# A batch's DFT folded fully on POOL and taken through DRAM, its load moved ahead of a weight load, and the last stores split over two queues

## The chip, the cores and the metric

The kernel runs on one core of a Trainium2 chip. The metric is the device time of one execution in microseconds; for the kernel before, the median of four runs is 630.72 us (630.26 to 631.77). Five engines work side by side: TensorE (PE), VectorE (DVE), ScalarE (ACT), GpSimd (POOL) and SyncE (SP, which only issues DMAs here). Each takes its own instructions strictly in the program's order and waits on semaphores for the others.

## The reference

```python
x: float32 [8, 3008, 256]
y = fft(fft(x, axis=1), axis=2).real            # real part of a 2-D DFT, per batch
g = y @ w_gate;  v = y @ w_val                  # 256 -> 1536, over 24064 tokens
out = (gelu(g) * v) @ w_out                     # 1536 -> 256, float32
```

## The kernel before, in words

The eight batches go one after the other. Each has two parts: a DFT that prepares the tokens, and the feed-forward part (FFN).

**FFN.** The tokens of a batch are worked on in three chunks (512, 512 and 481 columns). A column stands for a token and for its mirror token, since the real part of the DFT splits into an even part E and an odd part O that the two share with opposite signs. For each chunk and each of the 12 slices of 128 of the hidden width there is one *slot*; a batch has 36 slots (NS), the program 288, and a slot takes about 2.1 us. In a slot TensorE does the gate matmuls (L659 into ps_g), those of the value (L659 into ps_v) and up to two pieces of four output matmuls (L748) that belong to the chunk before. ACT applies GELU (L675, L684), DVE combines the values (L703, L719, L721), and POOL multiplies the mirrored half (L723 into h_sb), one slot later. An output piece needs h_sb of four slices: its last piece for the first 128 columns of a chunk comes three slots after the chunk's last slice, two after the L723 of that slice. ACT copies finished output tiles (L768) and SP stores them, four DMAs a tile (L653).

**DFT of the next batch.** It runs in the slots of the batch before. The input rows are loaded in forward and in mirrored order (the mirrored ones by indirect gathers that POOL issues, L158) and *folded* on POOL: sums of forward and mirrored rows and channels (L215, L216, L219). Five pieces, PIECES, cover the 17 row groups. For batches 2 to 7 the fold works in f32 on x_raw, writes ab_sb, and two more operations (L223, `combine`) give the sum and the difference as bf16 in eo_sb. Then comes `s1t`: 17 matmuls of 256 columns with G as weights (L545), ACT writes the result to S_sb (L548), SP writes S_sb to DRAM in two DMAs (L556) and reads it back as Z_sb in another arrangement (L567). From Z_sb, `tp_y`, `tp_e` and `tp_o` (L611, L581) make E and O of the batch in EO_sb, and `tp_rows` copies one row through DRAM (yrow, L625 and L627).

Batches 0 and 1 are different (`half = b < 2`): their rows are cast to bf16 by the load (xb), and the fold writes its sums directly into eo_sb, without `combine`. Their first stage is `s1`, 34 matmuls of 96 columns (L504) into A_sb (ACT, L510), and `ch` puts the halves together with 24 matmuls of 256 columns against the signed identity II (L526), six evictions into Z_sb (ACT, L531). Batch 0 does all this before and early in its own slots, batch 1 in slots 6 to 33: fold operations in POOL slots 6 to 10 and 14 to 18, `s1` in slots 13, 14 and 16 to 21, `ch` and the `tp` functions spread over 22 to 33.

**Order.** The order is written out by hand: `opening` emits the loads and the first DFT; `plan` fills two tables, `pool` (fold operations) and `fill` (everything else beside the FFN), by slot; `feed` walks the slots. In a slot the order is gate, last slot's second gate part, value, the first of two output pieces, the slot's POOL operations, last slot's second value part with its L723, the second output piece, the slot's `fill` entries. For the first chunk, `sooner` in `feed` says in which slot its first six output pieces go.

In `opening` POOL issues, in order, the casts of x(0), eight casts of gate and value weights (w_raw), two casts of the output weight (Wo_sb, L428), and then the six casts and gathers of x(1) into xb (L179, L158). SP's forward load of x(2) follows as soon as the buffer of x(0) is free.

**The end.** In the very last chunk each output tile of 128 tokens and one sign is copied alone: sign 0 by DVE (L761), stored by SP, sign 1 by ACT (L764), stored from ACT's own queue, two DMAs each.

Of the kernel before, what the change touches and what calls it, by code (L numbers as in the profile page):

```python
# [28 lines left out]
def kernel(  # L29
# [98 lines left out]
    def gelu_tile():  # L128
        return work([128, 2, TOK], BF16, "gelu", 5, "gelu_sb")
# [43 lines left out]

    xb, stage = {}, {}

    def cast_forward(b, j0, nj):
# [9 lines left out]

    def fold_ops(b, j0, nj, eng):
        st = {}  # L190
        half = b < 2

        def fwd(c0, pat):
            if b == 0 and j0 not in range(1, 9):
                return _sub(stage[0], [[C, nj]] + pat, (j0 - 9 if j0 else 8) * C + c0, part_num=NP)
            if half:
                return _sub(xb[b], [[C, nj]] + pat, j0 * C + c0, part_num=NP)
            return _sub(raw_tile(FORWARD), [[C, nj]] + pat, j0 * C + c0, part_num=NP)

        def mir(c0, pat):  # L200
            if half:
                return _sub(xb[b], [[-C, nj]] + pat, (NJ + 16 - j0) * C + c0, part_num=NP)
            return _sub(raw_tile(MIRROR), [[-C, nj]] + pat, (16 - j0) * C + c0, part_num=NP)

        def ab(q, c0, pat):
            if half:
                return _sub(eo, [[C, nj]] + pat, j0 * C + q * 128 + c0)
            return _sub(st["ab"], [[C, nj]] + pat, q * 128 + c0)

        up, down = [[1, 127]], [[-1, 127]]  # L210

        def first():
            if not half:
                st["ab"] = ab_tile()
            eng.tensor_tensor(ab(0, 0, [[128, 2]]), fwd(0, [[128, 2]]), mir(0, [[128, 2]]), op=ALU.add)  # L215
            eng.tensor_tensor(ab(0, 1, up), fwd(1, up), mir(255, down), op=ALU.add)  # L216

        def second():
            eng.tensor_tensor(ab(1, 1, up), mir(1, up), fwd(255, down), op=ALU.add)  # L219

        def combine(g, op):
            def run():
                eng.tensor_tensor(  # L223
                    _sub(eo, [[C, nj], [1, 128]], j0 * C + g * 128),
                    ab(0, 0, [[1, 128]]), ab(1, 0, [[1, 128]]), op=op)
            return run

        if half:
            return [first, second]
        return [first, second, combine(0, ALU.add), combine(1, ALU.subtract)]  # L230
# [405 lines left out]
    def store(b, gi, sub, sign, osb_half, queue):  # L636
        segs = [c for c in cols[gi] if c[0] // 128 == sub]
        m = min(128, chunk_len[gi] - sub * 128)
        for off, k2, w in segs:
            p0 = off - sub * 128  # L640
            lo, hi = (1, w - 1) if sign and k2 == 0 else (0, w)
            if sign:
                t0 = T - k2 - N2 * (hi - 1)
                p1 = m - p0 - hi
            else:
                t0 = k2 + N2 * lo
                p1 = p0 + lo
            dst = ap_replace(
                out,
                ap=[[N2 * C, hi - lo], [1, C]],  # L650
                offset=out.offset + (b * T + t0) * C,
            )
            queue.dma_start(out=dst, in_=_sub(osb_half, [[1, C]], 0, part_start=p1, part_num=hi - lo))  # L653

    def ffn_work(b):
        cstate = {}
# [127 lines left out]
    def opening():  # L784
        stage[0] = stage_tile()
        xb[0] = xb_tile(0)
        for j0, nj, at in ((9, 8, 0), (0, 1, 8)):
            nc.sync.dma_start(
                out=_sub(stage[0], [[1, nj * C]], at * C),
                in_=ap_replace(x, ap=[[32 * C, NPX], [1, nj * C]], offset=x.offset + j0 * C))  # L790
        pool_consts()
        index_consts(0)
        cast_mirror(0, 9, 8)
        pool_consts2()
        cast_mirror(0, 5, 4)
        cast_forward(0, 1, 8)
        index_consts(1)
        cast_mirror(0, 0, 1)
        cast_mirror(0, 1, 4)
        for f0, n in ((0, 256), (256, 256), (512, 512), (1024, 512)):  # L800
            load_w(f0, n)
        for q in range(2):
            load_wo(q)
        xb[1] = xb_tile(1)
        cast_forward(1, 9, 8)
        cast_mirror(1, 9, 8)
        cast_forward(1, 0, 9)
        for j0, nj in ((5, 4), (1, 4), (0, 1)):
            cast_mirror(1, j0, nj)
        idle = gelu_tile()[:, 0, :]  # L810
        nc.vector.memset(one[:, 0:1], 1.0)
        sin_table()
        nc.vector.memset(idle, 0.0)

        def warm(n):

            ps = psum("o")
            for _ in range(n):
                nc.tensor.matmul(ps[:, :], idle[:, 0:128], idle[:, :], start=True, stop=True)  # L819

        def fold_piece(j0, nj):
            for f in fold_ops(0, j0, nj, nc.vector):
                f()

        vec_consts()
        vec_fills()
        warm(7)
        g_phases()
        t_columns()
        t_phases()  # L830
        g_rows(9, 7)
        t_reduced()
        vec_consts2()
        identities()
        cw_phases()
        g_ends()
        cw_magnitude()
        vec_fills2()
        g_rows(1, 8)
        t_sin()  # L840
        cw_sin()
        gelu_table()
        warm(6)
        fold_piece(9, 4)
        s1(0, 2, 0)()
        s1(0, 2, 1)()
        warm(8)
        fold_piece(13, 4)
        cw_rest()
        fold_piece(5, 4)  # L850
        s1(0, 1, 0)()
        s1(0, 1, 1)()
        warm(2)
        fold_piece(0, 1)
        s1(0, 3, 0)()
        s1(0, 3, 1)()
        fold_piece(1, 4)
        t_write()
        s1(0, 0, 0)()
        s1(0, 0, 1, "V")()  # L860
        minus = []
        make_w(0, 0, 256, m_at=minus, tag="o")()
        ch(0, 0)()
        ch(0, 1, "V")()
        make_w(1, 0, 256, m_at=minus, tag="g")()
        tp_e(0, 0, 0, "V", tag="v")()
        tp_e(0, 0, 1, "A", tag="v")()
        minus[0]()
        minus[1]()
# [7 lines left out]
    def plan():  # L877
# [16 lines left out]
        for i, f in enumerate(early):  # L894
            at(fill, (7, 8, 9, 10, 11, 12, 13, 14, 15, 16)[i], f)

        ops = []
        for piece in PIECES:
            ops += fold_ops(1, *piece, nc.gpsimd)
        slot_of = [6, 7, 8, 9, 10, 14, 15, 16, 17, 18]  # L900
        for s, f in zip(slot_of, ops):
            at(pool, s, f)
        s = 12
        for jg, piece in ((2, 1), (1, 2), (0, 3), (3, 4)):
            for g in range(2):
                s = max(s + 1, slot_of[2 * piece + 1] + 2)
                at(fill, s, s1(1, jg, g))
        last1 = s
        for k, s in ((0, 8), (1, 9), (2, 9)):
            at(fill, s, lambda k=k: load_part(2, k, (load_forward,)))  # L910
        for k, s in ((0, 18), (1, 19), (2, 19)):
# [8 lines left out]
                if i % each == each - 1:  # L920
                    at(fill, s + 1, tp_rows(b, i // each))

        items = []
        for gi in range(NG):
            items += [ch(1, 2 * gi), ch(1, 2 * gi + 1), tp_y(1, gi), tp_e(1, gi), tp_o(1, gi)]
        spread(1, items, last1 + 1, NS - 3)
        for b in range(2, B):
            s0 = (b - 1) * NS
            ops = []
            for j0, nj in PIECES:  # L930
                ops += fold_ops(b, j0, nj, nc.gpsimd)
            per = len(ops) // 5
            first, n = {2: (s0 - 13, 29), 3: (s0 - 19, 30)}.get(b, (s0 - 22, 32))
            slot_of = [first + i * n // len(ops) for i in range(len(ops))]
            for s, f in zip(slot_of, ops):
                at(pool, s, f)
            if b + 1 < B:
                for k, piece in ((0, 1), (1, 3), (2, 4)):
                    at(fill, slot_of[piece * per + 1] + 1, lambda b=b, k=k: load_part(b + 1, k))
            s = s0 - 9  # L940
            for i, (jg, piece) in enumerate(((2, 1), (1, 2), (0, 3), (3, 4))):
                ready = slot_of[piece * per + per - 1] + 2
                for g in range(2):
                    s = max(s + 1, ready)
                    at(fill, s, s1t(b, jg, g))
                if i == 2:
                    at(fill, s + 1, z_write(b, 0, 12))
                if i == 3:
                    at(fill, s + 1, z_write(b, 12, 4))
            at(fill, s + 2, z_read(b))  # L950
            items = []
            for gi in range(NG):
                items += [tp_y(b, gi), tp_e(b, gi), tp_o(b, gi)]
            assert s + 7 < s0 + NS - 10
            spread(b, items, s + 7, s0 + NS - 3)
        return fill, pool

    def feed():
# [6 lines left out]
        pend, before = [], None  # L965

        first = works[0]
        sooner = {6: [first[0]], 7: [first[3]], 10: [first[1]], 11: [first[4]], 13: [first[2]], 14: [first[5]]}
        works[0] = first[6:]
        for i, (parts, fc) in enumerate(blocks):  # L970
            if fc == 0 and i:
# [58 lines left out]
```

## Time and profile before

| | |
|---|---|
| median of the runs | 630.72 us (630.26 to 631.77) |
| the profiled execution | 631.84 us, of which its span is 630.1 us |
| TensorE busy, granted clock | 619.6 us (98% of the span), 1.00 |
| DVE, ACT, POOL busy | 578.4, 430.7, 494.5 us |
| L526 on TensorE (ps_dft<-II, A_sb) | 44 recorded, 20 of them of batch 0 |
| L504 on TensorE (from eo_sb) | 68, 34 of them of batch 1 |
| L545 on TensorE (from eo_sb, G) | 102, 17 for each of batches 2 to 7 |
| bytes moved by DMA | 63.83 MB, mean 101 GB/s |

A profile row gives the start in the span, the busy time, the engine, the line of the kernel, the operation, output<-inputs with their shapes, and the count; in brackets the idle time just ahead and what ended it. Matmuls overlap in a pipeline, so a row's busy time is longer than the distance to the next. The first slices of the span are the opening, slot 0 starts at 20.6 us.

### The profile page before, as it was taken

The page shows a single profiled execution, that of the slowest core. Times are in us where ns is not written, and L with a number is a line of the kernel's source. Part 1 is how long each engine was busy: PE and PEld are TensorE (multiplying, and loading weights), DVE is VectorE, ACT ScalarE, POOL GpSimd, SP SyncE. Part 2 cuts the span into 40 slices and gives each one's busy share as a digit, 9 for nine tenths or more (in the row PEclk, how much of TensorE's full clock was granted, in tenths as well). Part 3 has the DMA queues.
Part 4 walks back from the last instruction along what each step waited for, and adds up shares of the span by engine and source line. Part 5 has one row for each costly group of instructions (what it writes and reads, how often), then busy time and mean ns, then how long its engine had stood idle before and what let it go on. Part 6 is the DMA issues. An engine that isn't in the chain of part 4 may idle for free.

```text
span 630.1 us, 13007 instructions
## 1 busy us (share of the span) xinstructions
PE 619.6 (98%) x4284; PEld 408.7 (65%) x4284; DVE 578.4 (92%) x941; ACT 430.7 (68%) x848; POOL 494.5 (78%) x500
## 2 busy tenths in 40 slices
PE   8999999999999999999999999999999999999997
PEld 4456666666666666666666666666666666666666
DVE  7589889999899999999999999999999999999992
ACT  5867777767766667666776767766776766666661
POOL 8358889989997998879998799969988555555551
PEclk9999999999999999999999999999999999999999
DMA  9951525534454352632636335633222332221123
GB/s 179 222 98 27 149 63 144 137 103 138 119 146 107 90 140 68 169 113 72 154 93 157 93 68 138 153 91 104 56 54 54 89 95 55 52 52 38 43 51 80
DMA packets 52505, 63.83 MB, mean 101 GB/s; under 512 B 7783, under 2 KB 48218, under 8 KB 50042
## 3 DMA queue, kind: packets, MB, share of 16 engines
q1 hardware_dynamic: 45238, 47.23, 29.3%
q0 software_dynamic: 6608, 15.29, 11.3%
q8 instruction: 33, 0.54, 0.4%
q10 hardware_dynamic: 592, 0.49, 0.3%
q14 instruction: 34, 0.28, 0.2%
HBM read 38.86 MB, written 29.38 MB: 108 GB/s over the span
## 4 chain that ended last, share of the span: by engine, by line
PE 93%; DVE 2%; ACT 2%; issue 1%; DMA 1%; POOL 0%; POOLq 0%; DVEq 0%; ACTq 0%
PE ps_o L748 38%; PE ps_g L659 29%; PE ps_v L659 19%; PE ps_dft L545 2%; PE ps_dft L581 2%; PE ps_o L819 1%; DMA EO_sb<-yrow 1%; PE ps_dft L526 1%; PE ps_dft L442 1%; ACT gelu_sb L675 1%; PE ps_dft L611 0%; PE ps_g L748 0%; PE ps_v L389 0%; ACT gelu_sb L684 0%; DVE v_sb L721 0%
## 5 line engine op out<-in xcount | busy, mean ns | idle before, releaser
L723 POOL TENSOR_TENSOR h_sb<-gelu_sb,v_sb 128x512 bf16<-128x512 bf16 (+1 forms) x280 | 319.6, 1144 | 103.7 <-DVE v_sb L721 93.6
L748 PE MATMUL ps_o<-Wo_sb,h_sb 128*128 128x256 bf16 (+1 forms) x2232 | 334.6, 273 | 0.0
L748 PEld LDWEIGHTS <-h_sb 128*128 128x128 bf16 (+1 forms) x2304 | 228.8, 100 | 111.4 <-POOL h_sb L723 1.2
L675 ACT ACTIVATE gelu_sb<-ps_g 128x512 bf16<-128x512 f32 (+1 forms) x288 | 169.5, 589 | 98.1 <-PE ps_g L659 97.7
L659 PE MATMUL ps_g<-EO_sb,W_sb 128*128 128x512 bf16 (+1 forms) x864 | 231.1, 376 | 1.6 <-ACT gelu_sb L684 1.1
L703 DVE SCALAR_TENSOR_TENSOR ve_sb<-EB_sb,yw,ps_v 128x512 f32<-128x512 bf16 (+1 forms) x280 | 206.2, 736 | 27.1 <-PE ps_v L659 25.9
L659 PE MATMUL ps_v<-EO_sb,W_sb 128*128 128x512 bf16 (+1 forms) x576 | 214.0, 376 | 0.5 <-DVE W_sb L450 0.4
L719 DVE TENSOR_TENSOR h_sb<-gelu_sb,ps_v 128x512 bf16<-128x512 bf16 (+1 forms) x280 | 189.6, 677 | 1.1 <-ACT gelu_sb L684 0.7
L659 PEld LDWEIGHTS <-W_sb 128*128 128x128 bf16 x1440 | 136.6, 98 | 81.5 <-issue 2.1
L721 DVE SCALAR_TENSOR_TENSOR v_sb<-ve_sb,ps_v 128x512 f32<-128x512 f32 (+1 forms) x280 | 187.2, 669 | 0.0
L684 ACT ACTIVATE gelu_sb<-ps_g 128x512 bf16<-128x512 f32 (+1 forms) x288 | 169.0, 587 | 0.0
L768 ACT ACTIVATE out_sb<-ps_o 128x512 f32<-128x512 f32 x92 | 54.9, 597 | 34.5 <-PE ps_o L748 34.5
L223 POOL TENSOR_TENSOR eo_sb<-ab_sb 94x512 bf16<-94x512 f32 (+1 forms) x60 | 66.6, 1110 | 0.1
L591 ACT ACTIVATE EO_sb<-ps_dft 128x512 bf16<-128x512 f32 (+1 forms) x44 | 26.0, 590 | 23.4 <-PE ps_dft L581 21.5
L548 ACT ACTIVATE S_sb<-ps_dft 96x512 bf16<-96x512 f32 x48 | 28.2, 587 | 11.3 <-PE ps_dft L545 11.3
L219 POOL TENSOR_TENSOR ab_sb<-x_raw,x_raw 94x508 f32<-94x508 f32 (+1 forms) x30 | 33.0, 1099 | 0.0
L216 POOL TENSOR_TENSOR ab_sb<-x_raw,x_raw 94x508 f32<-94x508 f32 (+1 forms) x30 | 32.9, 1097 | 0.0
L545 PE MATMUL ps_dft<-eo_sb,G 94*96 94x256 bf16 x102 | 19.2, 274 | 0.1
L158 POOL DMA_INDIRECT x_raw<-in_x_dram,idx x18 | 17.0, 942 | 2.8 <-issue 0.8
L581 PE MATMUL ps_dft<-TP,Z_sb 128*128 128x128 bf16 (+1 forms) x184 | 17.9, 218 | 0.7 <-DVE Z_sb L533 0.7
L581 PEld LDWEIGHTS <-Z_sb 128*128 128x128 bf16 x192 | 14.6, 98 | 2.8 <-DVE Z_sb L533 1.4
L158 POOL DMA_INDIRECT xb<-in_x_dram,idx x8 | 7.7, 966 | 9.0 <-DMA w_raw<-in_moe_w_gate_dram 7.0
(148 smaller groups left out, 191.9 us busy)
## 6 DMA issues: line engine op xcount, KB each, us to landing
out_dram<-out_sb SPq DMA_DIRECT2D x361, 64.0 KB
x_raw<-in_x_dram SPq DMA_DIRECT2D x10, 768.0 KB
Z_sb<-z SPq DMA_DIRECT2D x6, 768.0 KB
z<-S_sb SPq DMA_DIRECT2D x6, 576.0 KB
EB_sb<-yrow SPq DMA_DIRECT2D x14, 128.0 KB
x_raw<-in_x_dram SPq DMA_DIRECT2D x2, 640.0 KB
z<-S_sb SPq DMA_DIRECT2D x6, 192.0 KB
EB_sb<-yrow SPq DMA_DIRECT2D x7, 120.2 KB
```

Source lines behind the costliest of these rows:

```text
L219: eng.tensor_tensor(ab(1, 1, up), mir(1, up), fwd(255, down), op=ALU.add)
L223: eng.tensor_tensor(_sub(eo, [[C, nj], [1, 128]], j0 * C + g * 128), ab(0, 0, [[1, 128]]), ab(1, 0, [[1, 128]]), op=op)
L581: nc.tensor.matmul(ps[:, o : o + n], st["Z"][:, pair, g * 128 : g * 128 + 128], _sub(TP, [[1, n]], g * 128), start=True, stop=True)
L659: nc.tensor.matmul(ps[:, :n], W[nm, part][:, fs], src, start=start, stop=stop, **kw)
L675: nc.scalar.activation(gl[:, 0, :n], pg[:, :n], AF.Gelu)
L684: nc.scalar.activation(_sub(gl, [[-1, n]], TOK + n - 1), pg[:, :n], AF.Gelu)
L703: nc.vector.scalar_tensor_tensor(ve[:, :n], EB_bufs[b][:, c0 : c0 + n], yw[:, fc : fc + 1], pv[:, :n], op0=ALU.mult, op1=ALU.add)
L719: nc.vector.tensor_tensor(st["h"][:, fc, 0, :n], gl[:, 0, :n], pv[:, :n], op=ALU.mult)
L721: nc.vector.scalar_tensor_tensor(_sub(vv, [[-1, n]], n - 1), ve[:, :n], 2.0, pv[:, :n], op0=ALU.mult, op1=ALU.subtract)
L723: nc.gpsimd.tensor_tensor(st["h"][:, fc, 1, :n], gl[:, 1, :n], vv[:, :n], op=ALU.mult)
L748: nc.tensor.matmul(pso[:m, half], st["h"][:, fc, sign, h0 : h0 + m], Wo_sb[:, fc, :], start=(fc == 0 and not (first and sign)), stop=(fc = ...
L768: nc.scalar.activation(_sub(osb, [[1, 2 * C]], 0, part_num=m), pso[:m, :], AF.Copy)
```

## The change

It has four parts. Batch 1 keeps its bf16 input (`cast = b < 2`) but takes the way of the later batches: a full fold with ab_sb in f32 and `combine` on POOL, `s1t`, the write to DRAM and the read back, and the `tp` functions; its POOL operations get a slot list of their own, 4 to 18, `s1t` lies in slots 13 to 18, 20 and 21, the z writes in 19 and 22, the read in 23, and the `tp` functions in slots 27 to 39, the last of them in the first slots of its own FFN. In `opening` the six loads of x(1) go ahead of the two of Wo_sb. The first two output pieces of chunk 0 move from slots 6 and 7 to 8 and 9. And in `store`, every segment but the first of a tile goes to SP's queue, which matters only where the queue was ACT's, in the last chunk.

```diff
     def fold_ops(b, j0, nj, eng):
         st = {}
-        half = b < 2
+        half, cast = b < 1, b < 2
 ...
-            if half:
+            if cast:
                 return _sub(xb[b], [[C, nj]] + pat, j0 * C + c0, part_num=NP)
 ...
     def store(b, gi, sub, sign, osb_half, queue):
-        for off, k2, w in segs:
+        for i, (off, k2, w) in enumerate(segs):
 ...
-            queue.dma_start(out=dst, in_=_sub(osb_half, [[1, C]], 0, part_start=p1, part_num=hi - lo))
+            (nc.sync if i else queue).dma_start(out=dst, in_=_sub(osb_half, [[1, C]], 0, part_start=p1, part_num=hi - lo))
 ...
-        for q in range(2):
-            load_wo(q)
         xb[1] = xb_tile(1)
         cast_forward(1, 9, 8)
         cast_mirror(1, 9, 8)
         cast_forward(1, 0, 9)
         for j0, nj in ((5, 4), (1, 4), (0, 1)):
             cast_mirror(1, j0, nj)
+        for q in range(2):
+            load_wo(q)
 ...
-        ops = []
-        for piece in PIECES:
-            ops += fold_ops(1, *piece, nc.gpsimd)
-        slot_of = [6, 7, 8, 9, 10, 14, 15, 16, 17, 18]
 ...
-                at(fill, s, s1(1, jg, g))
-        last1 = s
 ...
-        items = []
-        for gi in range(NG):
-            items += [ch(1, 2 * gi), ch(1, 2 * gi + 1), tp_y(1, gi), tp_e(1, gi), tp_o(1, gi)]
-        spread(1, items, last1 + 1, NS - 3)
-        for b in range(2, B):
+        for b in range(1, B):
 ...
+            if b == 1:
+                slot_of = [4, 4, 5, 5, 6, 6, 7, 7, 8, 8, 9, 13, 13, 14, 15, 15, 16, 17, 17, 18]
 ...
-            if b + 1 < B:
+            if 1 < b < B - 1:
 ...
-            s = s0 - 9
+            s = s0 - 9 if b > 1 else 12
 ...
+            if b == 1:
+                spread(b, items, s + 6, s + 18)
+                continue
 ...
-        sooner = {6: [first[0]], 7: [first[3]], 10: [first[1]], 11: [first[4]], 13: [first[2]], 14: [first[5]]}
+        sooner = {8: [first[0]], 9: [first[3]], 10: [first[1]], 11: [first[4]], 13: [first[2]], 14: [first[5]]}
```

More of the change, by code (lines that the diff above doesn't have):

```diff
@@ L200, in mir @@
         def mir(c0, pat):
-            if half:
+            if cast:
                 return _sub(xb[b], [[-C, nj]] + pat, (NJ + 16 - j0) * C + c0, part_num=NP)
@@ L895, in plan @@
             at(fill, (7, 8, 9, 10, 11, 12, 13, 14, 15, 16)[i], f)
-        ops = []
-        for piece in PIECES:
-            ops += fold_ops(1, *piece, nc.gpsimd)
-        slot_of = [6, 7, 8, 9, 10, 14, 15, 16, 17, 18]
[L901 to L906, printed above, removed]
-                at(fill, s, s1(1, jg, g))
-        last1 = s
         for k, s in ((0, 8), (1, 9), (2, 9)):
```

## The prediction

> **What bounds the kernel now.** I read the page's engine shares first, then the chain that ended last, then the timelines of TensorE, POOL and SP from 14 to 110 us, where the second batch is prepared, and the last 5 us.
>
> ```profile
> PE 619.6 (98%) x4284; PEld 408.7 (65%) x4284; DVE 578.4 (92%) x941; ACT 430.7 (68%) x848; POOL 494.5 (78%) x500
> PE   8999999999999999999999999999999999999997
> PEclk9999999999999999999999999999999999999999
> PE 93%; DVE 2%; ACT 2%; issue 1%; DMA 1%; POOL 0%; POOLq 0%; DVEq 0%; ACTq 0%
> ```
>
> TensorE is full in nearly every slice, at full clock, and carries 93% of the chain. So a matmul removed anywhere after the start is worth its spacing, unless another engine then keeps TensorE waiting. Busy times of single matmuls overlap; I take the distance from one group's start to the next.
>
> ```profile
> 42.46 0.81 PE L659 MATMUL ps_g<-EO_sb,W_sb 128*128 128x512 bf16 x3
> 50.21 0.34 PE L504 MATMUL ps_dft<-G,eo_sb 94*128 94x96 bf16 x4
> 50.38 0.81 PE L659 MATMUL ps_g<-EO_sb,W_sb 128*128 128x512 bf16 x3
> 77.93 0.60 PE L526 MATMUL ps_dft<-II,A_sb 128*128 128x256 bf16 x4
> 78.37 0.77 PE L659 MATMUL ps_g<-EO_sb,W_sb 128*128 128x481 bf16 x3
> 79.82 0.60 PE L748 MATMUL ps_o<-Wo_sb,h_sb 128*128 128x256 bf16 x4
> 82.68 0.22 PE L611 MATMUL ps_dft<-TP,Z_sb 128*4 128x128 bf16 x1
> 99.99 0.38 PE L545 MATMUL ps_dft<-eo_sb,G 94*96 94x256 bf16 x2
> 100.21 0.80 PE L659 MATMUL ps_g<-EO_sb,W_sb 128*128 128x512 bf16 x3
> ```
>
> Read off: a group of four L504 takes 0.17 us (50.21 to 50.38), four L526 0.44 (77.93 to 78.37), two L545 0.22 (99.99 to 100.21). Slots are told apart by their L659 gate groups: slot 10 starts at 42.46, slot 14 at 50.38, slot 26 at 78.37.
>
> **The change part by part.**
>
> *Matmuls of the second batch.* Removed: 34 L504 in eight groups, six of four (0.17) and two of five (0.21, 68.42 to 68.63), 1.44 us; and 24 L526 in six groups of 0.435, 2.61 us. Added: 17 L545 at 0.11, 1.87 us. Net 2.2 us off TensorE. ACT loses six Z evictions of 0.596 us; its eight remaining grow from 0.488 to 0.587. ACT is 68% busy, so I count nothing. The Trainium skill, page "TensorE: Matmul & The Clock Gate", section "Back-to-back issue gap", gives about 81 ns for a 128-column matmul in a stream with weight loads; by it the 34 small ones are worth an estimated 2.75 us and the sum falls 1.3 us further. The rows say 43 ns, and I follow them.
>
> *The order of the casts.* In before the two Wo_sb casts stand ahead of x(1). By issue time plus time to landing (DMA view), the last weight cast landed at 28.2, Wo_sb at 29.8 and 31.3, then x(1): 33.7, 35.5, 37.5, 38.6, 39.5, 39.7. One queue, in order, saturated until 39.7. Exchanged, x(1) lands 3.1 us earlier: POOL's first fold, which stood until 35.74, can start at about 32.6, and Wo_sb lands at about 38.2 and 39.7. POOL's issue of the second Wo_sb cast has to wait until the weight cast of eight issues before has landed (28.2), before the fold could start. Range of the start: 32.6 to 35.7 (no gain at all, if the hardware queue's load for x(2), issued at 15.1, sets the pace).
>
> *First output matmuls two slots later.* Four L748 (0.44 us) leave slots 6 and 7 and join 8 and 9. Slot 8 waited 0.42 us for a DVE weight cast (PE wait L659 <- DVE W_sb L450). That cast moves up by only 0.44 while TensorE arrives 0.87 earlier, so the wait becomes 0.86; the added 0.44 in slot 8 brings it level, and in slot 9 it lies under the 0.2 us wait of L581 for Z_sb. Zero. They need the first Wo_sb half near 39.9, 1.7 us after it lands. Without that cover each microsecond of lateness costs one.
>
> *POOL.* Fold of the second batch: 10 more combining adds, and 94x508 adds from bf16 into f32, which before does not show.
>
> ```profile
> 35.92 1.14 POOL L216 TENSOR_TENSOR eo_sb<-xb 94x508 bf16<-94x508 bf16 x1
> 37.02 1.14 POOL L219 TENSOR_TENSOR eo_sb<-xb 94x508 bf16<-94x508 bf16 x1
> 44.17 1.16 POOL L723 TENSOR_TENSOR h_sb<-gelu_sb,v_sb 128x512 bf16<-128x512 bf16 x1 [3.64 <-ACT gelu_sb L684]
> 50.34 1.16 POOL L723 TENSOR_TENSOR h_sb<-gelu_sb,v_sb 128x512 bf16<-128x512 bf16 x1 [0.69 <-DVE v_sb L721]
> 75.80 1.25 POOL L219 TENSOR_TENSOR ab_sb<-x_raw,x_raw 94x508 f32<-94x508 f32 x1
> 78.14 1.27 POOL L223 TENSOR_TENSOR eo_sb<-ab_sb 94x512 bf16<-94x512 f32 x1
> ```
>
> Spacings: add 1.11 (bf16) to 1.23 (f32 rows); I take 1.12, since the mixed L723 (bf16 and f32 in, 512 wide) runs at 1.16, near the bf16 row. Combine 1.235, small add 0.17, L723 1.13, gather 1.1. Now POOL's queue in the new order. From 32.6: two pieces of 0.17 + 2 x 1.12 + 2 x 1.235 = 4.88 end at 42.4, the third's adds and first combine at 46.0. So the first L723 starts at 46.0 instead of 44.17, but the fourth still waits for DVE at 50.34: caught up. Then in order a combine, the fourth piece, the small last piece, three gathers and L723 for slots 13 to 22 without a gap: L723 of slot 15 starts at 59.85, slot 18 at 65.1, slot 22 at 73.0. With the next batch's first adds (1.4, 1.23) in slots 23 and 24, the L723 of slot 24 ends at 79.05; in before it ended at 78.2. L748 of slot 26 needs it for its fourth weight load, near 80.05 in before. By then TensorE is ahead by 1.56: three L526 groups 1.31, the L611 and two L581 groups that moved behind slot 26 (0.25 with the gap before it, 0.22, 0.22), less 0.43 for L545 over L504. It asks at 78.49 and waits 0.6 us. This is the one cost I put on the path: +0.6. With the f32 price and a start at 35.7 the same sum ends at 82.1, a wait of 3.6; with half a microsecond less on the chain it is zero. The eo pieces are ready in time: the fourth at 59.85 for slot 17 near 60.2, the last at 65.1 for 66.6. Five gelu buffers and four v buffers take two slots of lateness. The Trainium skill, page "GPSIMD Engine Reference", section "3.1 Elementwise — side-by-side cycle accounting", counts about 2.6 cycles for each element of a two-input operation and knows no difference of types; as an estimate that is 1.10 us for 508 elements, POOL would be done at 78.2, and the sum would be 0.6 us lower. The f32 rows contradict it by 0.15 us.
>
> *The trip through DRAM.* New on SP, in slots 19, 22 and 23: two z writes and a Z read, each in line with the stores.
>
> ```profile
> 52.72 23.90 SPq L653 DMA_DIRECT2D out_dram<-out_sb  x16
> 142.84 0.35 SPq L567 DMA_DIRECT2D Z_sb<-z  x1
> 626.14 0.38 ACT L764 ACTIVATE out_sb<-ps_g 128x256 f32<-128x256 f32 x1 [2.24 <-PE ps_g L748]
> 626.56 1.12 ACTq L653 DMA_DIRECT2D out_dram<-out_sb  x2
> ```
>
> The read stands behind the four stores of slot 23, which ended at 76.62 in before (0.6 us each); 0.3 earlier now, so it is issued near 76.35. After the issue at 142.84 DMA traffic ended near 147.6, after the one at 209.31 near 213.3: 4.0 to 4.8 us. Z_sb is there at 80.4 to 81.2. It waits for no z write any more (slot 22, some 5 us before), and the z writes wait for S_sb of slots 18 and 21 with only the later stores of slots 20 and 23 behind them. L611 of slot 27 asks at 82.68 - 1.56 - 0.44 + 0.6 = 81.3. Zero, with nothing to spare; this is what is late next: with the POOL wait gone, it takes up to 0.6 of what that frees. The SP queue behind it (yrow, the row copies for EO_sb in slots 31, 35, 40) serves the next batch at slots 36, 48, 60, four slots or more later.
>
> *Last stores.* After the last L764 ACT issues two stores in 1.12 us. Now SP, free at 626.45, issues the second beside it: the last issue ends 0.55 us earlier, and the span with it (0 if the landing of the stores, not the issue, is the limit).
>
> **Sum.** -2.2 + 0.6 - 0.55 = -2.15. The profiled execution took 631.84 (span 630.1) and would take 629.7. It lies 1.1 above the median of the runs shown, 630.72; carried over to that, 628.6.
>
> **Rivals.** *POOL is late all the way.* If x(1) comes no earlier (start 35.7, adds at 1.12), slot 24's L723 ends at 81.2, TensorE waits 2.7, and it nets to 630.7; with f32 prices 631.6. For it: the first megabytes share the DMA engines with x(2). Against: the saturated queue lands in order of issue.
> *Z late, slower.* If the read takes not 4 to 5 but 8.5 us to land, at 84.85 against 80.7 asked, TensorE stands 4.2 us in slot 27 (POOL's 0.6 lies within it): -2.75 + 4.2 = +1.4, 632.1. It turns slower than before from a landing 7.1 us after issue. For it: a 1 KB row copy that SP issued at 159.16 was on the chain for 4.02 us. Against: both readable Z reads.
> *More comes off.* In the windows table TensorE is idle for 0.62 us from 36 to 46 and 0.65 from 46 to 55. If the moved L748 and L545 fill all of that, and POOL keeps up, -2.75 - 1.27: 626.7. Against: most of these waits end with a DVE result.
>
> **How the numbers follow.** Forecast 0.58, POOL late 0.22, Z late 0.14, more 0.06. A measurement tells about 0.2%, 1.26 us, from no change. Forecast and more lie below it: faster 0.64; POOL late within it, 0.22; Z late above, 0.14. The forecast's own range is 627.6 to 629.4 (POOL wait gone and 0.4 of the idle 1.27 filled; POOL wait 1.4). With POOL late at its upper price the range is 627.6 to 631.6, which leaves out Z late and more, 0.20.
>
> **What would show it.** Right: no L526 after 60 us; 17 more L545; POOL's first fold starting near 32.6; an L748 wait on POOL h_sb of about half a microsecond near 79; L611 near 81 without a long wait; one store for each L764 on ACT's queue. Wrong: POOL's fold still starting near 35.7, waits of L748 on h_sb of over 2 us, TensorE waiting for Z_sb, or for Wo_sb near 40.

## The result

The changed kernel takes 629.29 us (median of 49 runs, 628.14 to 630.67), the kernel before 630.28 us (75 runs): a ratio of 0.9982, 95% interval 0.9977 to 0.9988, or 1.1 us less (0.8 to 1.5). The forecast was 2.1 us less (628.6 against 630.72). The direction holds, and half of the gain is missing. The time of 629.29 lies inside the forecast's own range (627.6 to 629.4), but with some luck, since before itself took 0.4 us less here than the 630.72 that the range was counted from: as a gain the range is 1.3 to 3.1 us, and 1.1 lies just below it.

Every execution has a span, from its first to its last instruction, and a time outside it. They split the result in two parts that the prediction had not told apart (the 102 executions of before are those that ran beside the experiments):

| | before | after | difference |
|---|---|---|---|
| median span (102 and 51 executions) | 628.7 | 627.1 | -1.6 |
| median time outside the span | 1.77 | 2.21 | **+0.44** |

The time outside varies by only 0.03 us (standard deviation) from run to run of one kernel, so the 0.44 is no noise. The span varies more, by 0.7 to 0.9 us in the changed kernel and 0.9 to 1.4 in before, and the -1.6 is less certain for it: in the round in which both kernels ran side by side again (experiment 5) the medians are 628.3 and 627.4, -0.9. A part of the variation lies in the opening: slot 0 starts between 18.6 and 21.3 us in the profiles of this study. So positions below are counted from slot 0. Lines of the changed kernel have numbers one higher than before (L724 for L723).

The page of the changed kernel, engine shares and chain:

```profile
PE 615.2 (98%) x4243; PEld 405.1 (64%) x4243; DVE 578.0 (92%) x941; ACT 428.3 (68%) x842; POOL 504.8 (80%) x510
PE 91%; DMA 2%; ACT 2%; POOL 1%; DVE 1%; issue 1%; SPq 0%; POOLq 0%; ACTq 0%; DVEq 0%
```

TensorE's busy time is 4.4 us less, at the same 98% of the span, but its idle time grew from 10.5 to 13.3 us and its share of the chain fell from 93% to 91%: DMA and POOL took it. TensorE's timeline shows where:

```profile
59.47 0.38 PE L546 MATMUL ps_dft<-eo_sb,G 94*96 94x256 bf16 x2 [0.23 <-POOL eo_sb L224]
78.83 0.28 PE L749 MATMUL ps_o<-Wo_sb,h_sb 128*128 128x256 bf16 x1 [0.87 <-POOL h_sb L724]
78.95 0.77 PE L660 MATMUL ps_g<-EO_sb,W_sb 128*128 128x481 bf16 x3
81.49 0.22 PE L612 MATMUL ps_dft<-TP,Z_sb 128*4 128x128 bf16 x1 [0.45 <-DMA Z_sb<-z]
```

Before had none of these three waits. POOL's timeline gives the reason for the second:

```profile
32.95 0.21 POOL L216 TENSOR_TENSOR ab_sb<-xb 94x8 f32<-94x8 bf16 x1 [1.96 <-DMA xb<-in_x_dram,idx]
33.14 1.13 POOL L217 TENSOR_TENSOR ab_sb<-xb 94x508 f32<-94x508 bf16 x1
34.24 1.14 POOL L220 TENSOR_TENSOR ab_sb<-xb 94x508 f32<-94x508 bf16 x1
35.45 2.49 POOL L224 TENSOR_TENSOR eo_sb<-ab_sb 94x512 bf16<-94x512 f32 x2
46.57 4.53 POOL L724 TENSOR_TENSOR h_sb<-gelu_sb,v_sb 128x512 bf16<-128x512 bf16 x4
77.62 1.15 POOL L724 TENSOR_TENSOR h_sb<-gelu_sb,v_sb 128x512 bf16<-128x512 bf16 x1
```

The fold starts at 32.95, when x(1) has landed, and POOL then has no gap, but for up to 0.3 us at each of its three load issues, up to the product of slot 24, which ends at 78.77. SP's timeline gives the reason for the third: the read of Z_sb was held back by the landing of the second z write, 8 us after its issue.

```profile
69.10 0.52 SPq L557 DMA_DIRECT2D z<-S_sb  x1
77.19 0.35 SPq L568 DMA_DIRECT2D Z_sb<-z  x1
```

The end of ACT's timeline shows one store behind the last copy instead of two:

```profile
624.63 0.38 ACT L765 ACTIVATE out_sb<-ps_g 128x256 f32<-128x256 f32 x1 [2.24 <-DMA out_dram<-out_sb]
625.05 0.50 ACTq L654 DMA_DIRECT2D out_dram<-out_sb  x1
```

How much POOL's slack shrank is read from the table of windows (PE, PEld, DVE, ACT, POOL busy), first before, then after:

```profile
33.00:51.00 18.00, 17.26 (x113) 9.51 (x111) 16.02 (x27) 12.92 (x26) 10.17 (x12) 1.00 0.36 69
51.00:80.00 29.00, 28.47 (x228) 19.36 (x227) 26.36 (x41) 22.53 (x46) 25.91 (x28) 1.00 0.37 96
80.00:110.00 30.00, 30.00 (x219) 20.35 (x218) 27.15 (x43) 22.18 (x45) 27.52 (x27) 1.00 0.40 108
```
```profile
33.00:51.00 18.00, 17.22 (x109) 9.68 (x108) 16.38 (x28) 13.28 (x26) 17.76 (x18) 1.00 0.41 59
51.00:80.00 29.00, 27.86 (x196) 18.32 (x195) 26.41 (x42) 20.50 (x40) 28.23 (x32) 1.00 0.51 141
80.00:110.00 30.00, 29.55 (x216) 19.62 (x215) 27.18 (x42) 21.70 (x45) 29.36 (x30) 1.00 0.44 116
```

POOL was idle for 13.4 of these 77 us before and is for 1.7 after.

### The profile page after: what moved, and what is told of

It is laid out like the page before. It is cut to its first block, busy times and chain, and to the rows that moved or that the text cites. A ratio compares the mean times of both kernels' runs of the same rounds, so it can differ in the third digit from the quotient of the medians.

```text
span 628.5 us, 12943 instructions
## 1 busy us (share of the span) xinstructions
PE 615.2 (98%) x4243; PEld 405.1 (64%) x4243; DVE 578.0 (92%) x941; ACT 428.3 (68%) x842; POOL 504.8 (80%) x510
## 4 chain that ended last, share of the span: by engine, by line
PE 91%; DMA 2%; ACT 2%; POOL 1%; DVE 1%; issue 1%; SPq 0%; POOLq 0%; ACTq 0%; DVEq 0%
PE ps_o L749 38%; PE ps_g L660 29%; PE ps_v L660 19%; PE ps_dft L546 2%; PE ps_dft L582 2%; DMA xb<-in_x_dram,idx 1%; DMA Z_sb<-z 1%; DMA out_dram<-out_sb 1%; ACT gelu_sb L676 1%; PE ps_o L820 1%; POOL h_sb L724 1%; PE ps_dft L443 1%; PE ps_dft L612 0%; ACT gelu_sb L685 0%; POOL eo_sb L224 0%
## 5 line engine op out<-in xcount | busy, mean ns | idle before, releaser
L724 POOL TENSOR_TENSOR h_sb<-gelu_sb,v_sb 128x512 bf16<-128x512 bf16 (+1 forms) x280 | 319.6, 1145 | 94.4 <-DVE v_sb L722 88.4
L224 POOL TENSOR_TENSOR eo_sb<-ab_sb 94x512 bf16<-94x512 f32 (+1 forms) x70 | 77.7, 1112 | 0.4
L549 ACT ACTIVATE S_sb<-ps_dft 96x512 bf16<-96x512 f32 x56 | 32.9, 587 | 13.6 <-PE ps_dft L546 13.5
L546 PE MATMUL ps_dft<-eo_sb,G 94*96 94x256 bf16 x119 | 22.5, 274 | 0.2 <-POOL eo_sb L224 0.2
L546 PEld LDWEIGHTS <-G 94*96 94x96 bf16 x119 | 13.0, 124 | 1.2 <-issue 0.4
```

The lines of the kernel that those rows point to most:

```text
L224: eng.tensor_tensor(_sub(eo, [[C, nj], [1, 128]], j0 * C + g * 128), ab(0, 0, [[1, 128]]), ab(1, 0, [[1, 128]]), op=op)
L546: nc.tensor.matmul(ps[:96, q * C : (q + 1) * C], G[:, j, :], _sub(eo, [[1, C]], j * C), start=(j == js[0]), stop=(j == js[-1]))
L724: nc.gpsimd.tensor_tensor(st["h"][:, fc, 1, :n], gl[:, 1, :n], vv[:, :n], op=ALU.mult)
```

## The experiments

Theory: TensorE does lose 2.2 us of matmuls, but POOL without a gap and behind it the Z read hold it up in slots 26 to 28, and the end gives less than counted. Rivals: the removed matmuls are worth less; the early slots pay; the waits are not what costs.

The table gathers all runs. Positions are the start of a slot in the profiled execution, against the profile of before, both from their slot 0 (us); "outside" is the median time outside the span. A last matmul is to be read with care, since two waits behind slot 60, which before has too, differ from execution to execution by up to 2 us (experiment 5).

| run | median us | ratio (95%) | slot 26 | slot 28 | slot 40 | last matmul | outside |
|---|---|---|---|---|---|---|---|
| changed kernel | 629.29 | 0.9982 (0.9977-0.9988) | -1.50 | -0.35 | -0.43 | -0.66 | 2.21 |
| the same again | 629.66 | 0.9986 (0.9972-0.9999) | -1.94 | -1.11 | -1.20 | -2.49 | 2.25 |
| output weight first | 633.36 | 1.0046 (1.0030-1.0063) | +2.00 | +2.62 | +2.54 | +2.45 | 1.96 |
| before, order alone | 630.15 | 0.9998 (0.9987-1.0010) | -0.33 | -0.33 | -0.33 | -0.62 | 1.78 |
| one store queue | 630.38 | 0.9993 (0.9982-1.0005) | -1.47 | +0.03 | -0.06 | -0.90 | 2.18 |
| fold 2 later | 629.65 | 0.9984 (0.9974-0.9994) | -1.81 | -0.71 | -0.82 | -1.43 | 2.07 |
| Z users later | 631.45 | 1.0002 (0.9985-1.0019) | -1.94 | -1.89 | -0.35 | -0.63 | 2.22 |
| fold 2 and first Z user later | 629.21 | 0.9979 (0.9967-0.9990) | -1.95 | -2.60 | -2.46 | -2.81 | 2.07 |
| all loads later | 636.09 | 1.0087 (1.0071-1.0104) | -1.42 | +2.26 | +5.37 | +4.75 | 2.05 |
| two loads later | 629.44 | 0.9987 (0.9971-1.0003) | -1.60 | -1.71 | -1.24 | -2.54 | 2.22 |
| two loads later, read earlier | 629.45 | 0.9984 (0.9967-1.0000) | -1.80 | -2.21 | -1.40 | -2.27 | 2.21 |
| fold 2, loads, read | 630.32 | 0.9983 (0.9964-1.0001) | -1.94 | -2.35 | -0.90 | -1.21 | 2.07 |
| before, 13 memsets | 631.85 | 1.0016 (1.0004-1.0029) | +0.01 | +0.01 | +0.01 | +1.47 | 2.24 |

**1. The order of the casts.** First undone in the changed kernel:

```diff
+        for q in range(2):
+            load_wo(q)
         xb[1] = xb_tile(1)
 ...
-        for q in range(2):
-            load_wo(q)
```

> The changed kernel with one part undone: the two output-weight casts stand ahead of x(1) again. Theory (POOL is the chain from x(1)'s landing to slot 24): the first fold starts some 3 us later, near 36.0, POOL has no gap from there, the product of slot 24 ends near 81.8 instead of 78.8, the wait of the output matmuls of slot 26 on h_sb grows from 0.87 to near 3.9, and the wait for Z_sb (0.45 us) disappears in it. Time near 629.3 + 2.5 = 631.8 us, ratio to before 1.0024. Rival (the x(1) load is not what starts the fold, or the removed matmuls are simply worth less than 2.2 us): the start moves by less than 0.5 us and the time stays within 0.3 us of 629.3.

The fold started at 36.05, as forecast, and POOL had no gap. The price was 1.6 us over the theory's 631.8, since the lateness struck in slot 14 already. ACT's, then TensorE's timeline:

```profile
50.85 0.60 ACT L676 ACTIVATE gelu_sb<-ps_g 128x512 bf16<-128x512 f32 x1 [3.42 <-POOL h_sb L724]
```
```profile
51.99 0.81 PE L660 MATMUL ps_g<-EO_sb,W_sb 128*128 128x512 bf16 x2 [2.73 <-ACT gelu_sb L685]
81.76 0.28 PE L749 MATMUL ps_o<-Wo_sb,h_sb 128*128 128x256 bf16 x1 [0.71 <-POOL h_sb L724]
```

POOL's first product came at 49.67. By then all five gelu buffers were full, ACT stood, and TensorE behind it. The lateness passed to TensorE through the buffers, and little was left for slot 26. So the early load is what makes the long fold possible: without it the change is slower than before.

Then alone, in the kernel before (the two `load_wo` calls behind x(1), `sooner` with 8 and 9):

> The kernel before with two parts of the change alone: x(1) ahead of the output weight, and the first two output pieces in slots 8 and 9 instead of 6 and 7. Theory (the early load pays only through the longer fold; the moved pieces and the later output weight cost nothing): no change, ratio 0.9995 to 1.0005, the first fold starts near 32.9 instead of 35.74, and slots 9 to 13 stand within 0.1 us of the kernel before, counted from slot 0. Rival (the late output weight or the fuller slots 8 and 9 cost part of the 2.2 us): TensorE waits near 40 us for Wo_sb, slots 9 to 13 are 0.5 to 1 us later, ratio 1.001 to 1.0015.

The fold started at 31.95, the time is that of before, and slots 9 to 13 stand at 0.00: the early load pays nothing by itself in the time, and neither the late output weight nor the fuller slots 8 and 9 cost anything. Most of the -0.33 from slot 15 on is a shorter wait for batch 0's Z_sb in slot 14 (0.26 us instead of 0.53).

**2. The last stores.**

```diff
-            (nc.sync if i else queue).dma_start(out=dst, ...)
+            queue.dma_start(out=dst, ...)
```

> The changed kernel with the last stores undone: all segments of a tile of the last chunk go to the queue that they had before. By the sum of the prediction this costs the 0.55 us that it counted: 629.85 us, ratio to before 0.9993. Theory from the two traces (the landing of the last stores and the closing waits of SP set the end, not the second issue): 0 to 0.1 us, ratio 0.9982 to 0.9984; the distance from the last copy of ACT to the last store data grows by some 0.4 us, and the distance from there to the end of the span shrinks by about as much.

The time cannot tell 0 from 0.55, the traces can. From the start of the last copy to the last byte stored it is 2.65 or 2.66 us in the three profiles of the kernel before and its variants and 2.66 here, against 2.29 to 2.33 in all with two queues: 0.35 gained. But from that byte to the end of the span it is 1.27 or 1.28 us in the kernel before and its variants and 1.56 to 1.60 in the changed kernel and all its variants, 1.56 here too. I expected this stretch to shrink here, and it did not: the 0.3 us belong to another part of the change. The two queues are worth 0.34 us (4.23 to 3.89 us from copy to end); something else takes 0.30 back.

The traces show what. SP closes the program with a list of waits for the DMAs' semaphores, one after the other in a fixed order, and one that finds its DMA already landed takes 0.06 us. The wait that is held up last ends 0.38 to 0.42 us after the last byte in all 14 profiles. In the three of before and its variants it is the last of the list; in all 11 of the changed kernel and its variants, this one too, five more stand behind it, which makes the 0.30 us. From the list to the end it is 0.84 us in all 14. Which part of the change gave the last store another place in the list was not tested.

**3. POOL's lateness and the Z read.** The fold of the third batch begins three slots later:

```diff
-            first, n = {2: (s0 - 13, 29), 3: ...
+            first, n = {2: (s0 - 10, 26), 3: ...
```

> The changed kernel with the fold of the third batch begun three slots later (POOL slots 26 to 50 instead of 23 to 50), so that two or three f32 adds of 1.23 us leave POOL's queue ahead of the product of slot 24. Theory (POOL's lateness and the Z read stand one behind the other): the wait of slot 26 on h_sb (0.87 us) is gone, the wait of slot 27 or 28 for Z_sb grows from 0.45 to near 1.4 because the read lands at the same moment, near 81.4, and the time stays: 629.3 us within 0.3, ratio 0.998. Rival (the two waits are independent, each has its own price): 1.0 us faster than the changed kernel, 628.3 us, ratio 0.9967.

As the theory had it: no wait on h_sb, and TensorE's timeline has

```profile
80.70 0.22 PE L612 MATMUL ps_dft<-TP,Z_sb 128*4 128x128 bf16 x1 [1.44 <-DMA Z_sb<-z]
```

so the Z read stands right behind POOL and takes what is freed. Now the users of Z_sb two slots later instead, `spread(b, items, s + 8, s + 20)`:

> The changed kernel with the functions that use Z_sb of the second batch two slots later each (slots 29 to 41 instead of 27 to 39); everything else stays. Theory: the wait for Z_sb (0.45 us by the wait view, 0.54 by the distance of slots) is gone and the wait on h_sb in slot 26 stays at 0.9: 0.5 us faster than the changed kernel, 628.8 us, ratio 0.9975. Rival (what is freed there is taken again by the next wait, on POOL or on the row copies of the first slots of the second batch): 629.3 us, ratio 0.998, with a new wait in the slots 28 to 42.

The rival. The Z wait is gone, slot 35 stands at -2.94, and then the row copy into EO_sb is late for the first slot of the second batch:

```profile
79.05 0.28 PE L749 MATMUL ps_o<-Wo_sb,h_sb 128*128 128x256 bf16 x1 [0.52 <-POOL h_sb L724]
99.41 0.58 PE L660 MATMUL ps_g<-EO_sb,W_sb 128*128 128x512 bf16 x2 [1.40 <-DMA EO_sb<-yrow]
```

Third, the later fold and only the first user of Z_sb one slot later (in `spread`, `if b == 1: s = max(s, s0 + 1)`):

> As the run with the fold of the third batch from slot 26, and beside it the first user of Z_sb alone one slot later (slot 28 instead of 27); the other functions of the second batch and its row copies stay in their slots. Theory: no wait on h_sb in slot 26, none above 0.2 us for Z_sb, and the row copies, still issued near 88, land near 93, a microsecond before slot 36 asks for them: 1.3 us faster than the changed kernel, 628.0 us, ratio 0.9962. Rival (the next link is late at once: the row copies into EO_sb, as in the run with all of these functions two slots later): a wait for EO_sb near 94 takes the gain again, 629.3 us, ratio 0.998.

In the profile all three waits are gone. Slot 60, which lies behind all that the change moved, stands at -2.56, and in the run of before's matmuls with the new order at -0.33: 2.2 us, so the removed matmuls are worth what was counted. (The last matmuls, -2.81 and -0.62, say the same, but hold the waits of experiment 5.) The time, 629.21, is not 628.0; its interval reaches from there to the changed kernel.

**4. Why the z write took 8 us.** With the later fold, the mirrored loads of x(2) in other slots:

```diff
-        for k, s in ((0, 18), (1, 19), (2, 19)):
+        for k, s in ((0, 23), (1, 28), (2, 28)):
```

> As the run with the fold of the third batch from slot 26, and beside it the three mirrored loads of x(2) later: slots 23, 28 and 28 instead of 18, 19 and 19. Theory (the second z write took 8 us to land because these loads held the DMA engines from 66 to 75 us): the write, issued near 68.4, lands in under 5 us, the Z read is issued right behind the stores of slot 23, near 74.8 instead of 76.35, lands near 79.2, and the wait for Z_sb falls from 1.44 to under 0.3: 1.2 us faster than the changed kernel, 628.1 us, ratio 0.9963. Rival (the write is slow by itself, 96 x 4 pieces of 512 bytes, whatever runs beside it): it lands after 8 us as before, the read is issued near 76.3, the wait for Z_sb stays near 1.4, 629.3 us, ratio 0.998.

POOL's, SP's and TensorE's timelines:

```profile
74.45 1.03 POOL L158 DMA_INDIRECT x_raw<-in_x_dram,idx  x1 [0.16 <-issue]
82.96 0.21 POOL L216 TENSOR_TENSOR ab_sb<-x_raw,x_raw 94x8 f32<-94x8 f32 x1 [4.96 <-DMA x_raw<-in_x_dram,idx]
```
```profile
68.77 0.51 SPq L557 DMA_DIRECT2D z<-S_sb  x1
75.23 0.47 SPq L568 DMA_DIRECT2D Z_sb<-z  x1
```
```profile
83.68 0.22 PE L612 MATMUL ps_dft<-TP,Z_sb 128*4 128x128 bf16 x1 [4.01 <-DMA Z_sb<-z]
```

The cause is right: the write's last 512-byte packet ended 2.1 us after the issue (70.83), against 7.5 in the changed kernel (76.59). But the read went out beside the first load and took 8.4 us instead of 4.3 (from its issue to the matmul that waited for it), and the load 8.5. Contention was moved from the write to the read. The rest of the 636.09 us came after the 4 us stall: TensorE's granted clock was 0.94 of full between 80 and 110 us, and POOL, whose fold stood 5 us for the load, was late again in slot 38 (a wait of 1.27 us). The Trainium skill, page "DMA: Bandwidth & Descriptors", section "Queues, rings and completion order", says that each DMA engine takes turns between its queues, a packet of several descriptors at a time. A write in pieces of 512 bytes that falls behind loads in pieces of 8,192 bytes in another queue, as here, would fit that; no run here shows the turns themselves.

So only two loads later, in slots 25 and 26, with the fold where the change has it:

> The changed kernel with two of the three mirrored loads of x(2) later (slots 25 and 26 instead of 19); the first stays in slot 18, the fold of the third batch in slot 23, the Z read in slot 23. Theory: two issues of about 1.2 us leave POOL's queue ahead of the product of slot 24, so the wait of slot 26 on h_sb is gone; the second z write, with only one load beside it, lands in under 4 us instead of 8, so the read is issued right behind the stores of slot 23, near 75.4 instead of 77.19; but it then meets the second load, which POOL issues near 77, and lands near 81 (between 79.5, alone, and 84, the 8.4 us that the read took beside a load in the run with all loads later), against 79.3 at which TensorE asks: a wait of 0.2 to 4, likely 1.7, and the time of the changed kernel, ratio 0.9985. Rival (what holds the read is its issue alone): it lands before 80, no wait, ratio 0.9965.

The write landed after 3.5 us (71.38), the read was issued at 74.33, and the second load at 78.72 no longer met it: a Z wait of 0.23 us, none on h_sb. Then the read behind the write in the same slot (`z_read` at `s + 1` for the second batch):

> As the run with two of the mirrored loads of x(2) in slots 25 and 26, and beside it the Z read one slot earlier, right behind the second z write. Theory: the write lands near 72 and the read is issued there, 5 us before the second load starts, and lands near 76 with nothing beside it; no wait for Z_sb, none on h_sb in slot 26, and 2.2 us of removed matmuls are all kept: 1.2 us faster than the changed kernel, 628.1 us, ratio 0.9965; slot 28 stands 2.2 us or more before the kernel before, counted from slot 0. Rival (the time is taken again behind, by the row copies that now meet the moved loads, or by the stores that queue behind the read): a wait for EO_sb near slot 36 or for out_sb near slot 24, ratio 0.998 or more.

The read was issued at 73.00 and had landed by 77.56, the waits of slots 26 to 28 are gone, and slot 28 stands at -2.21, as the theory had it. Then 0.8 us are lost up to slot 40; a part of it is seen in TensorE's timeline:

```profile
97.24 0.38 PE L546 MATMUL ps_dft<-eo_sb,G 94*96 94x256 bf16 x2 [0.52 <-POOL eo_sb L224]
```

Last, the later fold, the loads (slots 24 and 25) and the earlier read together:

> The changed kernel with three moves together: the fold of the third batch from slot 26 instead of 23, two of the three mirrored loads of x(2) in slots 24 and 25 instead of 19, and the Z read of the second batch one slot earlier, right behind the second z write. Theory (the waits of slots 26 and 27 are what keeps the changed kernel from its full 2.2 us in the span): no wait on h_sb in slot 26, none for Z_sb, none above 0.3 us on eo_sb in slots 30 to 40; the span's median 0.7 us under that of the changed kernel (627.1), 626.4, time 628.6 us, ratio 0.997. Rival (seen in the three runs that took the same waits away: the median span stayed at 627.2, because the execution then waits elsewhere or only starts to use its opening differently): median span 627.1 within 0.4, ratio 0.9982.

No wait up to slot 37, then one on the fold's own engine:

```profile
105.52 0.28 PE L749 MATMUL ps_o<-Wo_sb,h_sb 128*128 128x256 bf16 x1 [1.28 <-POOL h_sb L724]
```

The rival holds where loads were moved: their two issues, some 1 us each on POOL, now stand between 78 and 83 us, at the head of a stretch in which POOL is busy for 29.6 or 29.7 of 30 us (80 to 110), and a wait on POOL appears in slot 35 or 38. In this last run the product that slot 38 waits for starts 1.7 us later, counted from slot 0, than in the run with the later fold and the later first user. It is no rule for every wait taken away: that run moved no load, and it kept its gain up to slot 60 in its profile.

**5. The changed kernel again, beside these runs.**

> The changed kernel itself, on the same chip as the three others, with a profile of its own: ratio 0.998 within 0.001; the waits of slots 26 and 27 on h_sb and Z_sb together between 1.0 and 1.7 us.

Its profile shows the same wait on h_sb and none for Z_sb (expected: 1.0 to 1.7 us for both), and a last matmul at -2.49 instead of -0.66:

```profile
77.94 0.28 PE L749 MATMUL ps_o<-Wo_sb,h_sb 128*128 128x256 bf16 x1 [0.87 <-POOL h_sb L724]
```

So one execution of this kernel differs from the next by almost 2 us in what the waits cost, and the first profile was a poor one. Only 0.8 of the 1.83 us arose by slot 40, in slots 17 and 27. The other 1.1 us arose at the end of slots 66 and 100, which the change did not touch: there ACT waits for the row copy of a later batch (`yrow`), for 0.55 and 1.30 us in the first profile and not in the second, and TensorE then waits for ACT. Before has the same two waits (0.9 and 1.1 us). ACT's timeline of the first profile:

```profile
232.30 0.60 ACT L592 ACTIVATE EO_sb<-ps_dft 128x512 bf16<-128x512 f32 x1 [1.30 <-DMA EO_sb<-yrow]
```

This also bounds what the variants show: three runs in which these waits were gone or 0.23 us, and which lay within 0.25 us of each other (629.21, 629.44, 629.45; median spans 627.15 to 627.25), are not told apart from the changed kernel (627.1). None of them is a proven improvement; the one that ran beside this second run (fold 2 and first Z user later) had a median span of 627.15 against 627.40.

**6. The time outside the span.** In all runs it goes with the rows that the trace has for POOL: 823 or 824 rows, 1.77 us; 834, 1.96; 835, 2.05 to 2.07; 836, 2.18 to 2.25. It does not go in equal steps: ten rows more make 0.19 us, the next one 0.1 and the one after it 0.1 to 0.2. The test puts 13 idle instructions into the kernel before:

```diff
+        extra = const_pool.tile([128, 1], FP32, name="extra")
+        for i in range(13):
+            pool.setdefault(20 + i, []).append(lambda: nc.gpsimd.memset(extra, 0.0))
```

> The kernel before with 13 more instructions on POOL, memsets of 128 x 1 into a tile that nobody reads, one in each of the slots 20 to 32, where POOL had idle time. It asks what makes up the time outside the span, which is 1.76 us for the kernel before and 2.21 us for the changed kernel in all of their runs, while POOL has 823 recorded rows in the one and 836 in the other. Theory A (the number of POOL's instructions sets it): 2.1 to 2.3 us outside the span, the span itself as before (628.6), ratio 1.0007. Theory B (something else of the change sets it, the fold, the trip through DRAM or the order of the queues): 1.75 to 1.8 us outside, ratio 1.000.

```profile
69.76 0.11 POOL L969 MEMSET extra<- 128x1 f32 x1
```

Theory A holds: 2.24 us outside, with 836 rows, where the runs of before beside it had 1.78. The memsets take 0.1 us each and move no slot up to 60. The +1.47 of the last matmul comes from one wait in slot 100, again of ACT for a row copy (2.81 us). That the median span was 0.55 us longer too (629.65 against 629.1) the interval does not settle.

## Why the prediction was half right

- **Matmuls, -2.2: right.** Slot 26 stood at -1.50 and -1.94 in the two profiles of the changed kernel, forecast -1.56. That -1.50 comes so close is luck: it holds a loss of 0.44 in slot 17 and the 0.33 that the order alone brought, both left out of the forecast; -1.94 less 0.33 is -1.61. Without the waits the full 2.2 is there (slot 60 at -2.56 against -0.33).
- **Order of the casts, start at 32.6: right** (32.95; 31.7 to 33.9 in the others). That it decides was right as well, but the rival "POOL is late all the way" was priced by its wait in slot 26 alone (630.7 to 631.6). The gelu buffers, which "take two slots of lateness", do not take three: 633.36.
- **First output matmuls: right**, +0.07 and 0.00 in slots 9 to 13.
- **POOL's wait, +0.6: the place right, the size 1.04** in the profile (slot 26 to slot 27: -1.50 to -0.89, where 0.44 more should have come off). The price of the adds was right (1.10 from start to start). The third and fourth product did not wait for DVE, "caught up" never happened, and POOL ran without a gap from the load.
- **The trip through DRAM, zero: wrong.** The step that failed is "It waits for no z write any more". The write landed 7.5 us after its issue beside the loads of x(2), the read was issued at 77.19 for 76.35, and in that execution TensorE lost 0.54 us. In the second the write landed after 6.8 us, and there was no wait above 0.2 us.
- **eo pieces ready in time: nearly**; slot 17 waited 0.23 us and lost 0.44 in the first profile, 0.04 in the second.
- **Last stores, -0.55: too large.** The issue was not the limit: 0.34, and SP's closing waits take 0.30 more in the changed kernel, so the end as a whole gave 0.04.
- **"Carried over to that":** the sum took the time outside the span as fixed. It grew by 0.44, shown to go with POOL's instructions. With the 0.51 that the end did not give, this is the miss of about 1 us.

By medians it closes: -2.2 for the matmuls, -0.04 for the end and -1.6 of the span leave about 0.6 for the waits, as large as forecast; +0.44 outside makes -1.2, against the -1.1 of the ratio. The 0.6 is a remainder and not a measurement: with the -0.9 of the side-by-side round it would be 1.3. The rival "Z late" was wrong in size here, yet its 8.5 us for a read did occur, at 8.4, once a load was put beside it.

## What to carry to other kernels

Work moved to an engine with idle time uses up the slack that absorbed every later lateness: count the idle time that is left in the whole stretch, and the buffers between that engine and the bound one, since a late start reaches TensorE through full buffers before it does through data. Price a DMA by what else holds the engines while it lands, and expect a transfer that is moved to meet the next one. When an expected gain is a few tenths of a per cent, look at the time outside the span and at a second profile before explaining it.

## What was not expected of the hardware

- The time outside the span depends on the program: 1.77 to 2.25 us, with 823 to 836 rows on POOL, and 13 memsets of 0.1 us added 0.46 us. Why, no run here shows.
- A 192 KB write in 512-byte pieces landed after 2.1 us with none of the loads of x(2) beside it, 3.5 beside one and 7.5 beside three; a 768 KB read took 4.3 us, and 8.4 beside one load.
- The span's last stretch, from the last stored byte on, was 1.27 or 1.28 us in one program family and 1.56 to 1.60 in the other, whatever the queues of the stores: five more waits of SP, 0.06 us each, stood behind the one for the last store.
